# The first gate and value unit in two column halves, and the first weight clamp on GpSimd, in a chunked-scan and gated-MLP kernel

## The chip, the cores and the metric

The kernel runs on one core of a Trainium2 chip. A core has TensorE for matrix products (PE in the profile, its weight loads PEld), VectorE (DVE), ScalarE (ACT), GpSimd (POOL) and SyncE (SP), which here only issues DMAs. The metric is the device time of one execution in microseconds (us).

## What is computed

The reference is a decayed linear attention in chunks, followed by a gated MLP over its output. Cut to what matters:

```
cum = cumsum(log(clip(a)));  L = exp(cum_i - cum_j) * causal
y   = ((C B^T) * L) x  +  (C state) * exp(cum)          # within a chunk, and from the state carried in
state = exp(sum) * state + sum_j B_j x_j exp(cum_last - cum_j)
x   = y as [3072 tokens, 256]
out = (silu(x @ w_gate) * (x @ w_val)) @ w_out           # 256 -> 1536 -> 256
```

Batch 4, 8 heads, 768 positions, head size 32, state size 16; all data are float32.

## The kernel before

**Tiles and stages.** The 768 positions are cut into 6 blocks of 128 positions by 4 batches: 512 columns. A block's attention is done in pieces of Q=64 positions, so K=2 pieces in a block (the reference's chunk of 32 is not kept; the recurrence is the same). Its result y stands in four PSUM banks `y[2*q+g]`, where q is the piece and g the half of the 256 features, and is copied to SBUF as the MLP's moving operand: `xf` for block 0 (`x_whole`, line 510, four copies of 128x256), split into two parts for later blocks. The MLP works on 12 units f of 128 hidden features: `gate_val` (line 731) makes the bank `gv` of gate (m=0) and value (m=1) for a unit, `silu` and `product` combine them, `project` sums the output.

**Block 0** multiplies its first 9 units (WHOLE) in plain float32 with `w`, a rounded weight, instead of in three split products. A unit's weights come by DMA (`wg0r`, `wg1r`, ... 512 KB each) and go through six steps: `w_magnitude`, `w_sign`, `w_rest` on ScalarE; `w_range` (line 573, a clamp of 128x512), `w_shift` and `w_round` (lines 588 to 594) on VectorE. The unit can start when its `w_round` is done.

**Order of block 0.** Scan of the decays (`scan_spread`), scores S, `mix` (L times S, four instructions), `sums` (tile `st`, the new states, copied apart into T by ScalarE in `apart`), `values` (the part of y within a piece, in two groups g), `carried` (line 479, the part of y from the state, only for piece q=1), the four copies `xf`, and unit 0. `carried` needs the scan E and `weigh_c` (C times E, key `ce`). Between them TensorE runs `idle` products (tile `rest`, IDLE) so that it is not left without work.

**Block 1** is prepared meanwhile: its decays (`all`) are clamped by GpSimd in `clip_all`, written to DRAM by a DMA of ScalarE's queue (`write_all`, tile `clipped`) and read back, spread over partitions, as L and E by SP's queue (`load_aj`, `load_an`), along with `bc`, `xb` and the weights of units 7 to 11. VectorE scans L, weighs `xb` by it (`weigh_b`, key `bt`, one instruction for each batch) and TensorE then makes `st` and S of block 1.

**What sets the order.** The program is a list of steps (`add`), each with an engine and a cost, a rank, needs, and PSUM or SBUF slots that it takes. `Plan` simulates the engines with these costs and fixes each engine's instruction order once; at run time engines follow that order and wait on semaphores. `Ordered` holds each engine to program order. So a cost or rank that is changed for one step can move others. All recorded instructions carry line L199, a helper's; they are told apart by tiles.

Of the kernel before, what the change touches and what calls it, by code (L numbers as in the profile page):

```python
# [209 lines left out]
def scan_moe_kernel(ctx: ExitStack, tc, rows, decays, bc, xb, wgv, wo, cst, out):  # L210
# [635 lines left out]
    for n, ranks in enumerate(IDLE):  # L846
        for i, r in enumerate(ranks):
            need = [("idle", n, i - 1)] if i else [("idle", n - 1, len(IDLE[n - 1]) - 1)] if n else []
            if n:
                need = need + [(("S", 0, BATCH - 1), ("vals", 0), ("y", 0))[n - 1]]  # L850
            takes = [] if i or n else [("at", "rest")]
            c = T if n else P
            add("PE", 0.2133 * c / T, do(idle, n, i), r, need, takes=takes, uses=["rest"], gives=("idle", n, i), kind="r")


    for i in range(NW):
        r = due(0, i) - 1.0 if i < NF else due_sum(0, 2 * (i - NF)) - 1.0
# [4 lines left out]
        add([("Act", 0.57), ("DVE", 0.335)][: 1 + (i > 2)], None, do(w_rest, i), r - 4.5, [("mag", i), ("sign", i)], gives=("rest", i))
        add("Act", 0.57, do(w_sign, i), r - 5.4, [("mag", i)], gives=("sign", i))
        add("DVE", 0.6, do(w_shift, i), r - 4.2 if i else -1.05, [("range", i), ("sign", i)], gives=("shift", i))
        add("DVE", 0.6, do(w_round, i), r - 3.3 if i else -0.94, [("shift", i), ("rest", i), *([] if i else [("ce", 0)])], uses=[("raw", i)], gives=("round", i))
# [10 lines left out]
    add("Pool", 1.5, clip_all, 13.0, ["all", *(("bt", 0, b) for b in range(BATCH))], gives="clipped")  # L876
# [3 lines left out]
    for k in range(NB):  # L880
# [20 lines left out]
        if not k:  # L901
# [3 lines left out]
            for b in range(BATCH + 1):  # L905
                for i in range(2 if b < BATCH else 1):
# [7 lines left out]
                    need = [t, ("decays", 0), "dj"] + ([("scan0", b - last_one)] if i else []) + ([("M", 0, NP - 2)] if b == BATCH else [])  # L914
# [23 lines left out]
        for q in range(len(st)):  # L938
            add("Act", 0.5, do(apart, k, q), z + 4 + 0.5 * q, [("st", k, BATCH - 1), ("T", k)], uses=[st[q]], gives=("ap", k, q))
# [101 lines left out]
    for k in range(NB):  # L1041
        xs = [(t, k, i) for t in ("xh", "xl") for i in range(2 * K)]
        for f in range(NF):
# [10 lines left out]
            for m in range(2 if k < PAIR else 0):  # L1054
# [29 lines left out]
IDLE = [-9.0] * 22, [-1.45] * 4, [-1.35] * 2, [1000.0] * 3  # L1084
# [66 lines left out]
```

## Time and profile before

| | |
|---|---|
| three runs | 344.06, 345.26, 345.27 us; median 345.26 |
| profiled execution | 343.62 us, of which the span of instructions 341.9 us |
| PE busy | 337.3 us, 99% of the span |
| PEld, DVE, ACT, POOL busy | 260.7, 256.8, 173.4, 4.1 us |
| granted TensorE clock | 1.00 in every slice |
| bytes moved | 28.29 MB, mean 83 GB/s |

A busy share is an average over the kernel: TensorE is busy nearly all the time from 5.8 us on, VectorE without gaps worth the name only up to some 60 us, and the DMA engines mostly up to 39 us. The change lies in the first 20 us. So the timelines of the single engines in that stretch, and in block 1's preparation that follows it, are what is to be read, with the end of one instruction held against the start of the one that needs it.

### The profile page before, as it was taken

What the parts mean: (1) busy time and instruction counts of PE and PEld (TensorE: products, weight loads), DVE (VectorE), ACT (ScalarE), POOL (GpSimd) and SP (SyncE); (2) the same over time, 40 slices, a digit from 0 to 9 for tenths busy, and PEclk for the clock granted to TensorE, in tenths of its full rate; (3) what the DMA queues carried; (4) which work ended last, traced back from release to release, by engine and by line L of the source; (5) the groups of instructions that cost most, each with busy time, mean ns of one, the idle gap of its engine ahead of it and who ended that gap; (6) DMA issues with size and microseconds to landing.
All of it is one profiled execution on the core that took longest, in us unless ns stands there. A gap on an engine that the chain in (4) does not pass through costs nothing.

```text
span 341.9 us, 7521 instructions
## 1 busy us (share of the span) xinstructions
PE 337.3 (99%) x3165; PEld 260.7 (76%) x3165; DVE 256.8 (75%) x473; ACT 173.4 (51%) x315; POOL 4.1 (1%) x11
## 2 busy tenths in 40 slices
PE   8999999999999999999999999999999999999996
PEld 7544457888777888877788778877788888888895
DVE  6999999979697586553599943595869999856540
ACT  3696897372684552421344432323656556444542
POOL 1300000000000000000000000000000000000000
PEclk9999999999999999999999999999999999999999
DMA  7789535950000931000380107500010000000101
GB/s 257 259 263 334 176 120 173 220 172 1 0 2 15 254 108 62 0 2 2 124 191 0 63 2 206 105 2 2 3 63 0 0 3 0 0 0 2 51 11 63
DMA packets 10602, 28.29 MB, mean 83 GB/s; under 512 B 1096, under 2 KB 2120, under 8 KB 10568
## 3 DMA queue, kind: packets, MB, share of 16 engines
q1 hardware_dynamic: 10152, 27.57, 27.3%
q8 instruction: 25, 0.41, 0.5%
q10 hardware_dynamic: 416, 0.23, 0.2%
q14 instruction: 9, 0.07, 0.1%
HBM read 24.46 MB, written 3.35 MB: 81 GB/s over the span
## 4 chain that ended last, share of the span: by engine, by line
PE 89%; DMA 5%; ACT 4%; SPq 0%; issue 0%; ACTq 0%
PE gv L199 34%; PE po L199 30%; PE py L199 7%; PE y L199 5%; PE px L199 5%; DMA wg9r<-in_wgv 4%; PE pr L199 2%; PE pz L199 2%; PE S L199 2%; DMA bc<-in_bc 1%; PE st L199 1%; PE rest L199 1%; ACT sg L199 1%; ACT Cz L199 0%; ACT wg9r L199 0%; ACT wg2r L199 0%
## 5 line engine op out<-in xcount | busy, mean ns | idle before, releaser
L199 ACT CAST hh<-sg 128x512 fp32r<-128x512 f32 x70 | 43.4, 621 | 51.2 <-PE po L199 29.0
L199 DVE TENSOR_TENSOR hl<-sg,hh 128x512 fp32r<-128x512 f32 x72 | 49.3, 689 | 25.8 <-ACT hh L199 25.5
L199 ACT ACTIVATE sg<-gv 128x512 f32<-128x512 f32 x48 | 28.5, 595 | 50.6 <-PE gv L199 50.4
L199 DVE TENSOR_TENSOR sg<-gv,sg 128x512 f32<-128x512 f32 x48 | 32.8, 686 | 27.1 <-PE gv L199 27.0
L199 DVE TENSOR_TENSOR_SCAN L<-L,dj 128x520 f32<-128x520 f32 x20 | 23.9, 1227 | 0.0
L199 DVE TENSOR_TENSOR L<-S,L 128x512 f32<-128x512 f32 x24 | 15.0, 683 | 0.4 <-PE S L199 0.4
L199 PE MATMUL py<-xht,ws 128*128 128x512 f32 x48 | 14.8, 389 | 0.0
L199 ACT COPY ob<-po 128x512 f32<-128x512 f32 (+1 forms) x12 | 6.6, 551 | 13.1 <-PE po L199 12.5
L199 ACT ACTIVATE sg<-px 128x512 f32<-128x512 f32 x12 | 7.2, 598 | 10.9 <-PE px L199 10.9
L199 ACT ACTIVATE Cz<-bc,cs 128x512 f32<-128x512 f32 x12 | 8.0, 714 | 8.5 <-DMA bc<-in_bc 8.5
L199 DVE TENSOR_TENSOR mix<-mix 128x128 f32<-128x128 f32 (+1 forms) x36 | 11.9, 330 | 0.2
L199 DVE TENSOR_TENSOR ps<-py,ps 128x512 f32<-128x512 f32 x12 | 8.2, 686 | 4.8 <-PE py L199 4.8
L199 PEld LDWEIGHTS y<-L,xb 64*32 64x32 f32 x768 | 7.3, 105 | 5.0 <-issue 2.8
L199 PE MATMUL y<-L,xb 64*32 64x64 f32 x768 | 10.9, 222 | 0.0
L199 PEld LDWEIGHTS py<-xht,ws 128*128 128x128 f32 x48 | 9.0, 188 | 1.9
L199 PE MATMUL po<-hh,wo0h 128*128 128x512 f32 (+1 forms) x26 | 10.3, 394 | 0.0
L199 PE MATMUL po<-hh,wo2h 128*128 128x512 f32 (+1 forms) x26 | 9.9, 382 | 0.0
L199 PE MATMUL po<-hh,wo3h 128*128 128x512 f32 (+1 forms) x26 | 9.9, 381 | 0.0
L199 PE MATMUL y<-bc,T 32*64 32x64 f32 x352 | 9.9, 228 | 0.0
L199 PE MATMUL po<-hh,wo5h 128*128 128x512 f32 (+1 forms) x26 | 9.8, 378 | 0.0
L199 PE MATMUL po<-hh,wo4h 128*128 128x512 f32 (+1 forms) x26 | 9.8, 378 | 0.0
L199 PE MATMUL po<-hl,wo0h 128*128 128x512 f32 (+1 forms) x26 | 9.7, 375 | 0.0
(485 smaller groups left out, 875.0 us busy)
## 6 DMA issues: line engine op xcount, KB each, us to landing
L<-clipped SPq DMA_DIRECT2D x10, 520.0 KB, 9.7
xb<-in_xb SPq DMA_DIRECT2D x6, 768.0 KB, 5.1
bc<-in_bc SPq DMA_DIRECT2D x6, 512.0 KB, 9.2
out<-ob SPq DMA_DIRECT2D x11, 256.0 KB, 2.1
E<-clipped SPq DMA_DIRECT2D x5, 260.0 KB
wg0r<-in_wgv SPq DMA_DIRECT2D x1, 512.0 KB, 7.4
wg1r<-in_wgv SPq DMA_DIRECT2D x1, 512.0 KB
wg2r<-in_wgv SPq DMA_DIRECT2D x1, 512.0 KB, 4.2
```

The source lines that it names most:

```text
L199: ins = getattr(self.engine, name)(*a, **k)
```

## The change

Unit 0 of block 0 is multiplied by `gate_val_part` in four parts (gate or value, m, by column half q) with 256 columns each. A part of half q needs only the two copies of `xf` of that piece. The first part comes before `carried`, which now needs the first part to be issued, and the other three after it. `carried` no longer holds the banks of piece 0 (`y[:2]`). The second copy of piece 0 goes from ScalarE to VectorE. The clamp of `wg0` goes to GpSimd, ahead of `clip_all` there, which now needs it. E's scan and `weigh_c` come after `w_round` of unit 0 instead of before. Of the idle products there is one fewer before `sums` and one fewer between the two `values`, and the last three stand between the second `values` and unit 0's first part, no longer behind `carried`; costs and ranks of several steps are changed with it.

```diff
     def w_range(i):
         wf = part[i]["w"].bitcast(F32)
-        ve.tensor_scalar(wf, wf, *F32_RANGE, ALU.max, ALU.min)
+        (ve if i else ge).tensor_scalar(wf, wf, *F32_RANGE, ALU.max, ALU.min)
...
+    def gate_val_part(m, q):
+        if not q:
+            hid.setdefault((0, 0), {})["gv"[m]] = ps_mm.tile([P, T], F32, tag="mm", name=f"gv0_0_{m}")
+        t = hid[0, 0]["gv"[m]].rearrange("p (b i) -> p b i", b=BATCH)[:, :, piece(q)]
+        w = part[0]["w"].bitcast(F32).rearrange("p (a b c) -> p a b c", b=2, c=P)
+        for kc in range(2):
+            te.matmul(t, w[:, m, kc], x_part(whole[0], 2 * q + kc), start=not kc, stop=kc == 1, skip_group_check=True)
...
-        add("DVE", 0.335, do(w_range, i), r - 4.5 if i else -1.05, [("mag", i)] + ([("round", 0), *([("round", 1)] if i == 2 else [])] if i > 1 else []), gives=("range", i))
+        add(*(("DVE", 0.335) if i else ("Pool", 0.45)), do(w_range, i), r - 4.5 if i else -1.3, [("mag", i)] + ([("ce", 0)] if i == 1 else []) + ([("round", 0), *([("round", 1)] if i == 2 else [])] if i > 1 else []), gives=("range", i))
...
-    add("Pool", 1.5, clip_all, 13.0, ["all", *(("bt", 0, b) for b in range(BATCH))], gives="clipped")
+    add("Pool", 1.5, clip_all, 13.0, ["all", ("range", 0), *(("bt", 0, b) for b in range(BATCH))], gives="clipped")
...
-                    need = [t, ("decays", 0), "dj"] + ([("scan0", b - last_one)] if i else []) + ([("M", 0, NP - 2)] if b == BATCH else [])
+                    need = [t, ("decays", 0), "dj"] + ([("scan0", b - last_one)] if i else []) + ([("round", 0)] if b == BATCH else [])
...
-            add("PE", 0.135, do(carried, 0, b), -1, [("vals", 0), ("vals", 1), ("ce", 0), *steps], uses=uses, gives=("y", 0) if b == BATCH - 1 else ("y", 0, b), kind="f")
+            add("PE", 0.15, do(carried, 0, b), due(0, 0) + 0.05, [("gvp", 0), ("vals", 0), ("vals", 1), ("ce", 0), *steps], uses=[u for u in uses if u not in y[:2]], gives=("y", 0) if b == BATCH - 1 else ("y", 0, b), kind="f")
...
-                add([("Act", 0.62), ("DVE", 0.34)][i // 2 :][:1], None, do(x_whole, i), -0.9 + i / 10, [*(done if i > 1 else [("vals", 1)]), "xf"], uses=[y[i]], gives=("xf", i))
+                add([("Act", 0.62), ("DVE", 0.34)][min(i, 1) :][:1], None, do(x_whole, i), -1.0925 if i == 1 else -0.9 + i / 10, [*(done if i > 1 else [("vals", 1)]), "xf"], uses=[y[i]], gives=("xf", i))
...
+            for m, q in ((m, q) for q in range(K) for m in range(2 if not k and not f else 0)):
+                need = [("round", 0), ("xf", 2 * q), ("xf", 2 * q + 1), *([("gvp", m)] if q else []), ("idle", len(IDLE) - 1, len(IDLE[-1]) - 1)]
+                add("PE", 0.87, do(gate_val_part, m, q), r + q * 0.2 + m * 0.1, need + ([("y", 0)] if m and not q else []), takes=[] if q else [("mm", gv[m])], uses=[gv[m], "xf"] + ([("hh", "x")] if q else []), gives=gv[m] if q else ("gvp", m), kind="r")
...
-IDLE = [-9.0] * 22, [-1.45] * 4, [-1.35] * 2, [1000.0] * 3
+IDLE = [-9.0] * 22, [-1.45] * 3, [-1.35], [-1.3] * 3
```

On TensorE around unit 0, where `y_1_...<-bc` is `carried` and `gv_0_0`, `gv_0_1` are gate and value of unit 0, before:

```order
L199 MATMUL y_1_261<-bc_96,T_105 64x64
L199 MATMUL y_1_304<-bc_96,T_105 64x64
...
L199 LDWEIGHTS const-bfloat16-1.0
L199 MATMUL rest<-dn,const-bfloat16-1.0 128x512
...
L199 MATMUL gv_0_0_377<-xf,wg0w 128x512 x2
L199 MATMUL gv_0_1_392<-xf,wg0w 128x512 x2
L199 MATMUL gv_1_0_410<-xf,wg1w 128x512 x2
```

and now:

```order
L199 LDWEIGHTS const-bfloat16-1.0
L199 MATMUL rest<-dn,const-bfloat16-1.0 128x512
...
L199 MATMUL gv_0_0_344<-xf,wg0w 128x4x64 x2
L199 MATMUL y_1_259<-bc_96,T_105 64x64
L199 MATMUL y_1_301<-bc_96,T_105 64x64
...
L199 MATMUL gv_0_1_374<-xf,wg0w 128x4x64 x2
L199 MATMUL gv_0_0_344<-xf,wg0w 128x4x64 x2
L199 MATMUL gv_0_1_374<-xf,wg0w 128x4x64 x2
L199 MATMUL gv_1_0_403<-xf,wg1w 128x512 x2
```

The 16 products of `carried` moved from before the three idle products to behind the first half of the gate.

On VectorE from the end of `mix` to the rounding of unit 1 (`ISA` on a weight is `w_round`, the `SCALAR_TENSOR_TENSOR` on it `w_shift`, `bc_96<-bc_96,E_95` is `weigh_c`), before is - and now is +:

```order
-L199 SCALAR_TENSOR_TENSOR E_95<-a_0_202,dn 128x260
-L199 TENSOR_SCALAR wg0w<-wg0w 128x512
-L199 TENSOR_TENSOR bc_96<-bc_96,E_95 128x4x64
 L199 SCALAR_TENSOR_TENSOR wg0w<-wg0w,wg0r 128x512
 L199 ISA wg0w<-wg0r,wg0w 128x1024
...
+L199 COPY xf<-y_0_300 128x4x64
+L199 SCALAR_TENSOR_TENSOR E_95<-a_0_202,dn 128x260
+L199 TENSOR_TENSOR bc_96<-bc_96,E_95 128x4x64
```

E's scan and `weigh_c` went behind unit 0's rounding and a copy of `xf`, and the clamp of `wg0` is gone from this engine; the clamp of unit 1, the two other copies, `w_shift`, one cast and `w_round` of unit 1 follow in that order.

On SP, where L, E, `bc`, `xb` of block 1 are asked for, before is - and now is +:

```order
-L199 DMA L_367<-clipped 64x4x520 x2
-L199 DMA bc_389<-in_bc 128x1024
-L199 DMA xb_397<-in_xb 128x1536
+L199 DMA L_378<-clipped 64x4x520 x2
+L199 DMA E_379<-clipped 128x1x520
+L199 DMA bc_407<-in_bc 128x1024
+L199 DMA xb_412<-in_xb 128x1536
 L199 DMA wg7r<-in_wgv 128x1024
 L199 DMA wg8r<-in_wgv 128x1024
-L199 DMA E_368<-clipped 128x1x520
 L199 DMA wg9r<-in_wgv 128x1024
```

E of block 1 moved ahead of `bc`, `xb` and the weights of units 7 and 8.

## Rows read from the trace of the kernel before

**Rows 1.** The page, busy time, share of the span and instructions of each engine.

```profile
PE 337.3 (99%) x3165; PEld 260.7 (76%) x3165; DVE 256.8 (75%) x473; ACT 173.4 (51%) x315; POOL 4.1 (1%) x11
```

**Rows 2.** The timeline of PE around unit 0: start us, length us, engine, line, operation, tiles, shapes, count.

```profile
9.88 1.04 PE L199 MATMUL rest<-dn,const-bfloat16-1.0 128*128 128x512 bf16 x4
...
12.80 0.86 PE L199 MATMUL y<-L,xb 64*32 64x64 f32 x64
13.59 0.69 PE L199 MATMUL y<-bc,T 32*64 32x64 f32 x32
14.22 0.82 PE L199 MATMUL rest<-dn,const-bfloat16-1.0 128*128 128x512 bf16 x3
15.10 3.67 PE L199 MATMUL gv<-xf,wg0w 128*128 128x512 f32 x8
18.84 3.67 PE L199 MATMUL gv<-xf,wg1w 128*128 128x512 f32 x8
22.35 3.60 PE L199 MATMUL gv<-xf,wg2w 128*128 128x512 f32 x8
25.78 3.60 PE L199 MATMUL gv<-xf,wg3w 128*128 128x512 f32 x8
```

**Rows 3.** The timeline of DVE from `mix` to the rounding of unit 1 (the custom instruction is `w_round`), same columns; a length holds the drain, so that instructions overlap in the record.

```profile
9.45 2.46 DVE L199 TENSOR_TENSOR L<-S,L 128x512 f32<-128x512 f32 x4
11.83 0.69 DVE L199 TENSOR_TENSOR_SCAN E<-a,dn 128x260 f32<-128x260 f32 x1
12.43 0.41 DVE L199 TENSOR_SCALAR wg0w<-wg0w 128x512 f32<-128x512 f32 x1
12.74 0.42 DVE L199 TENSOR_TENSOR bc<-bc,E 128x256 f32<-128x256 f32 x1
13.08 0.70 DVE L199 SCALAR_TENSOR_TENSOR wg0w<-wg0w,wg0r 128x512 int32<-128x512 int32 x1
13.93 0.69 DVE L199 CUSTOM_DVE_ANT_0 wg0w<-wg0r,wg0w 128x1024 uint16<-128x1024 uint16 x1
14.54 0.75 DVE L199 COPY xf<-y 128x256 f32<-128x256 f32 x2
...
18.01 0.69 DVE L199 CUSTOM_DVE_ANT_0 wg1w<-wg1r,wg1w 128x1024 uint16<-128x1024 uint16 x1
```

**Rows 4.** The timeline of ACT in the same stretch, and the DMA of its queue (ACTq).

```profile
10.07 0.68 ACT L199 ACTIVATE wg0w<-wg0r 128x512 f32<-128x512 f32 x1 [2.02 <-DMA wg0r<-in_wgv]
10.78 0.70 ACT L199 ACTIVATE wg0r<-wg0r 128x512 int32<-128x512 int32 x1
11.72 0.62 ACT L199 ACTIVATE T<-st,cs 128x128 f32<-128x128 f32 x2 [0.24 <-PE st L199]
12.19 0.41 ACTq L199 DMA_DIRECT2D clipped<-all  x1
...
13.31 0.74 ACT L199 COPY xf<-y 128x256 f32<-128x256 f32 x2
```

**Rows 5.** The timeline of POOL, its work of more than 0.34 us.

```profile
0.88 0.66 POOL L199 TENSOR_SCALAR_AFFINE_SELECT rows<-const-float32-1.0 128x512 f32<-128x512 f32 x1 [0.39 <-POOLq L1140]
...
8.95 1.52 POOL L199 TENSOR_TENSOR xb<-xb,L 128x128 f32<-128x128 f32 x4 [7.13 <-DVE L L199]
10.66 1.49 POOL L199 TENSOR_SCALAR all<-all 128x384 f32<-128x384 f32 x1 [0.19 <-DMA all<-in_decays]
```

**Rows 6.** The timeline of SP's queue: when it asked for L of block 1 (two DMAs) and for the weights of unit 11, which the program lets go when L's second half has landed.

```profile
19.76 1.34 SPq L199 DMA_DIRECT2D L<-clipped  x2
...
28.65 0.33 SPq L199 DMA_DIRECT2D wg11r<-in_wgv  x1
```

**Rows 7.** Who SP's queue waited for: us in total, times, longest us.

```profile
SPq L199 <- DMA clipped<-all: 5.8, 1, 5.8
```

**Rows 8.** The timeline of DVE in block 1's preparation: the first scan of L, the first and the last `weigh_b`; in brackets the idle time before an instruction and who ended it.

```profile
28.90 1.24 DVE L199 TENSOR_TENSOR_SCAN L<-L,dj 128x520 f32<-128x520 f32 x1
...
31.60 0.29 DVE L199 TENSOR_TENSOR xb<-xb,L 128x128 f32<-128x128 f32 x1 [0.29 <-DMA xb<-in_xb]
...
38.35 0.29 DVE L199 TENSOR_TENSOR xb<-xb,L 128x128 f32<-128x128 f32 x1
```

**Rows 9.** The timeline of ACT there: the magnitudes of units 8 and 9, and block 1's states copied apart.

```profile
35.55 0.70 ACT L199 ACTIVATE wg8w<-wg8r 128x512 f32<-128x512 f32 x1 [0.69 <-DMA wg8r<-in_wgv]
...
38.21 0.68 ACT L199 ACTIVATE wg9w<-wg9r 128x512 f32<-128x512 f32 x1 [0.36 <-DMA wg9r<-in_wgv]
...
41.84 1.11 ACT L199 ACTIVATE T<-st,cs 128x128 f32<-128x128 f32 x4
```

**Rows 10.** The timeline of PE there: block 1's `st` and S.

```profile
39.61 0.86 PE L199 MATMUL st<-xb 64*32 64x64 f32 x64
...
42.31 1.85 PE L199 MATMUL S<-Cz,bc 32*64 32x128 f32 x64
```

**Rows 11.** The chain that ended last, one piece of it: start us, us, what.

```profile
43.01 1.16 PE S L199 x57
```

**Rows 12.** Busy time in a stretch: us from and to, its length, then PE, PEld, DVE, ACT, POOL busy us (instructions), granted PE clock, DMA share, GB/s.

```profile
13.60:17.00 3.40, 3.34 (x45) 1.73 (x41) 3.25 (x9) 2.28 (x5) 0.00 (x0) 1.00 0.98 354
```

**Rows 13.** The timeline near the kernel's end, two products of `project` with 256 columns in a row.

```profile
325.44 0.28 PE L199 MATMUL po<-hl,wo1h 128*128 128x256 f32 x1
...
325.55 0.28 PE L199 MATMUL po<-hh,wo1l 128*128 128x256 f32 x1
```

More of the change, by code (lines that the diff above doesn't have):

```diff
@@ L849, in scan_moe_kernel @@
             if n:
-                need = need + [(("S", 0, BATCH - 1), ("vals", 0), ("y", 0))[n - 1]]
+                need = need + [(("S", 0, BATCH - 1), ("vals", 0), ("vals", 1))[n - 1]]
             takes = [] if i or n else [("at", "rest")]
@@ L859, in scan_moe_kernel @@
         plan.marked[plan.ops[-1]] = ("sent", i)
-        add("Act", 0.565, do(w_magnitude, i), r - 5.5, [("raw", i)] + ([("xf", 2 * K - 1)] if i else []) + ([("rest", 1)] if i in (2, 3) else []), takes=[("sg" if i < NF else "w", ("w", i))], gives=("mag", i))
-        add("DVE", 0.335, do(w_range, i), r - 4.5 if i else -1.05, [("mag", i)] + ([("round", 0), *([("round", 1)] if i == 2 else [])] if i > 1 else []), gives=("range", i))
[L862 to L865, printed above, removed]
+        add("Act", 0.565, do(w_magnitude, i), r - 5.5, [("raw", i)] + ([("xf", 1 if i < 2 else 2 * K - 1)] if i else []) + ([("rest", 1)] if i in (2, 3) else []), takes=[("sg" if i < NF else "w", ("w", i))], gives=("mag", i))
+        add(*(("DVE", 0.335) if i else ("Pool", 0.45)), do(w_range, i), r - 4.5 if i else -1.3, [("mag", i)] + ([("ce", 0)] if i == 1 else []) + ([("round", 0), *([("round", 1)] if i == 2 else [])] if i > 1 else []), gives=("range", i))
+        add([("Act", 0.57), ("DVE", 0.335)][: 1 + (i > 2)], None, do(w_rest, i), r - 4.5 if i else -1.3, [("mag", i), ("sign", i)], gives=("rest", i))
+        add("Act", 0.57, do(w_sign, i), r - 5.4 if i else -1.2, [("mag", i)], gives=("sign", i))
+        add("DVE", 0.6, do(w_shift, i), r - 4.2 if i else -1.095, [("range", i), ("sign", i), *([("xf", 2 * K - 1)] if i == 1 else [])], gives=("shift", i))
+        add("DVE", 0.6, do(w_round, i), r - 3.3 if i else -1.094, [("shift", i), ("rest", i)], uses=[("raw", i)], gives=("round", i))
         early = WHOLE <= i < NF
@@ L933, in scan_moe_kernel @@
             n = len(bs)
-            add("PE", 0.11 if n == 1 else 0.787, do(sums, k, bs), -1.5 if not k else z + 3, [*(("bt", k, i) for i in bs), *([("st", k, more - 1)] if more else [] if k else [("spread", BATCH - 1, 1)])], takes=[] if more else [("at", i) for i in st], uses=st, gives=("st", k, b), kind="f", slack=SLACK, rows=1.0)
+            add("PE", 0.155 if n == 1 else 0.787, do(sums, k, bs), -1.5 if not k else z + 3, [*(("bt", k, i) for i in bs), *([("st", k, more - 1)] if more else [] if k else [("spread", BATCH - 1, 1)])], takes=[] if more else [("at", i) for i in st], uses=st, gives=("st", k, b), kind="f", slack=SLACK, rows=1.0)
             add("PE", 0.214 if n == 1 else 1.14, do(scores, k, bs), z + 3.5 if k else -1.9 + 0.1 * b, ([("Cz", k), ("st", k, BATCH - 1)] if k else apart_done) + ([("S", k, more - 1)] if more else []), takes=[] if more else [("at" if k else "mm", i) for i in S], uses=[*S, CZ], gives=("S", k, b), kind="f", slack=SLACK, rows=1.0)
@@ L938, in scan_moe_kernel @@
         for q in range(len(st)):
-            add("Act", 0.5, do(apart, k, q), z + 4 + 0.5 * q, [("st", k, BATCH - 1), ("T", k)], uses=[st[q]], gives=("ap", k, q))
+            add("Act", 0.5, do(apart, k, q), z + 4 + 0.5 * q, [("st", k, BATCH - 1), ("T", k), *([] if k else [("xf", 0) if q else ("rest", 0)])], uses=[st[q]], gives=("ap", k, q))
         for p in range(NP):
@@ L952, in scan_moe_kernel @@
             need = [("M", 0, p) for p in (2 * g, 2 * g + 1)]
-            add("PE", 0.45, do(values, 0, range(BATCH), (g,)), -1.4 + 0.1 * g, need, takes=[("mm", y[2 * q + g]) for q in range(K)], uses=[L, XB, *y], gives=("vals", g), kind="f")
+            add("PE", 0.62, do(values, 0, range(BATCH), (g,)), -1.4 + 0.1 * g, need, takes=[("mm", y[2 * q + g]) for q in range(K)], uses=[L, XB, *y], gives=("vals", g), kind="f")
         if k:
@@ L1053, in scan_moe_kernel @@
             gv = [("gv", k, f, m) for m in range(2)]
-            for m in range(2 if k < PAIR else 0):
+            for m, q in ((m, q) for q in range(K) for m in range(2 if not k and not f else 0)):
+                need = [("round", 0), ("xf", 2 * q), ("xf", 2 * q + 1), *([("gvp", m)] if q else []), ("idle", len(IDLE) - 1, len(IDLE[-1]) - 1)]
+                add("PE", 0.87, do(gate_val_part, m, q), r + q * 0.2 + m * 0.1, need + ([("y", 0)] if m and not q else []), takes=[] if q else [("mm", gv[m])], uses=[gv[m], "xf"] + ([("hh", "x")] if q else []), gives=gv[m] if q else ("gvp", m), kind="r")
+            for m in range(2 if k < PAIR and (k or f) else 0):
                 add("PE", c, do(gate_val, k, f, m), r + m * 0.1, need, takes=[("mm", gv[m])], uses=[gv[m], *([("x", k)] if k else ["xf", ("hh", "x")])], gives=gv[m], kind="r")
```

## The prediction

> **What bounds the kernel now.** The page first: TensorE is busy 99% of the span [rows 1], so the kernel is a queue of TensorE work, and a change in the first 20 us can only move the time by (a) when unit 0 starts, (b) gaps later in that queue. Second, TensorE's timeline around unit 0 [rows 2]: unit 0 starts at 15.10 and unit 1 at 18.84, a distance of 3.74, where units 2 and 3 lie 25.78 - 22.35 = 3.43 apart. So unit 1 came 0.31 late, and VectorE's timeline tells why: `w_round` of unit 1 runs from 18.01 to 18.70 [rows 3]. Unit 0 waits for the end of VectorE's list (clamp, `weigh_c`, shift, round, copies of `xf` to 15.29) [rows 3]. Third, where the queue stalls next: block 1's preparation. S of block 1 takes 1.85 us [rows 10], and the chain that ended last enters it only at 43.01 [rows 11], when ACT's copies of T (41.84 to 42.95) [rows 9] have freed the banks that `st` held. So some 43.01 - 42.31 = 0.7 us after S began, TensorE was still waiting for it. Whatever unit 0 gains must still be there at 43.01.
>
> **The head, part by part.** The changed order is laid on these durations; a hop between engines is taken as 0.1 us.
>
> GpSimd: the clamp of `wg0` can start when the magnitude ends, 10.07 + 0.68 = 10.75 [rows 4], so at 10.85. No row has a clamp of 128x512 on GpSimd. The bounds: not under 0.41, which is VectorE's own time for it [rows 3]; not over 1.49 x 512/384 = 1.99, which is `clip_all`, the same operation, by the element [rows 5]. I take 0.66, the pass over an unbroken 128x512 on the same engine [rows 5], because `clip_all` goes over 6 short rows and the clamp of `wg0` over one long one. Then the clamp ends at 11.51, before VectorE has done `mix` (11.83, where the next instruction starts [rows 3]): on this side it costs nothing. What it costs stands behind it in GpSimd's queue: `clip_all` starts at 11.5 instead of 10.66 and ends at 13.0 instead of 12.15, 0.85 later.
>
> One sentence from the notes for the near bound: the Trainium skill, GPSIMD Engine Reference, section 4.1 Engine selection, says that one-input work on GpSimd goes at about line rate; for 512 elements at its 1.2 GHz that would be an estimate of 0.43 us, and the sum below would be 0.2 us lower; no run here shows it.
>
> VectorE: shift at 11.83, round at 12.43, free at 13.03 (slots of 0.6, as 12.43 - 11.83 [rows 3]). The copy of `xf` needs the second `values`, which began at 12.80 and ended at 13.66 [rows 2]. Two idle products fewer stand ahead of it, 0.22 each (four fill 9.88 to 10.92 with their tail [rows 2]): it ends at 13.2. Copies to 13.65 (0.37 each [rows 4]). TensorE's three idle products (0.66) end at 13.9. So the first part starts at 13.9 instead of 15.10.
>
> TensorE from there: four parts of 3.43 / 4 = 0.86, and `carried`, 14.22 - 13.59 = 0.63 [rows 2], inside the unit: 13.9 to 14.75, `carried` to 15.4 (E's scan and `weigh_c` take 0.6 + 0.34 [rows 3] after 13.65 and are done at 14.6), second part to 16.25; the copies of piece 1 fall under it (15.5 to 16.2); end 17.95. Halves cost nothing extra by the row of `project`: two products with 256 columns start 0.11 apart [rows 13], though there in another number format; 0.02 us more on each of the 16 passes, which I take as the far bound, would be 0.3. Unit 1: VectorE is free at 16.2, then shift 0.6, cast 0.34, round 0.7 to 17.85. Unit 1 starts at 17.95 instead of 18.84: **0.9 us gained**, if nothing later waits.
>
> **What is late next.** `clip_all` feeds the DMA of `clipped`, which ACT's queue issued at 12.19, just after `clip_all` [rows 4, 5]; SP's queue waited 5.8 us for it before it could ask for L at 19.76 [rows 6, 7]. The DMA of `clipped` ran amid the fetches of the weights; I take it to land as much later as it is issued. So L is asked for at 20.6 instead of 19.76. L's second half landed at about 28.6 (unit 11's fetch is let go at 28.65 [rows 6]) and its scan started at 28.90, so it had no slack [rows 8]. Next, E stands ahead of `bc` and `xb` now. `xb` was waited for already: 0.29 us of idle time until 31.60 [rows 8]. E's 260 KB against L's 1040 KB in the 5 us or so before L's landing makes 1.2 us. So `xb` lands at 31.6 + 0.85 + 1.2 = 33.6. From the first to the end of the last `weigh_b` the new order has two scans (1.15 each), two products, shift and round (0.6 each), a clamp (0.33) and the four `weigh_b` (0.2 each), 5.8 us; before, the last began 38.35 - 31.60 = 6.75 after the first, with one scan more between [rows 8]. The last `weigh_b` is done at 39.4 and `st` starts at 39.5: about where it was before, 39.61 [rows 10]. TensorE, 0.9 early, waits 0.8 for it.
>
> Then S. ACT waited for the weights of units 8 and 9 (0.69 us until 35.55, 0.36 until 38.21 [rows 9]), and its chain to T begins with the latter: now 39.05 (E is ahead of them in both orders), while unit 8's, at 35.55 + 0.85 + 1.2 = 37.6, are done with by then. Five instructions of 0.5 to 0.6 follow (one fewer than before stands ahead of T) and T's 1.1: 39.05 + 2.8 + 1.1 = 42.95. T ended at 42.95 before [rows 9]. **Sum: the 0.9 us of the head is given back at `st`, and S goes on at 43.0 as before: 0.0 us**, within the errors of the hops. In the profiled execution that is 343.6 us (span 341.9); the median of the runs is 345.26, 1.64 above it, and I keep that distance: 345.2 us. Behind S both orders run TensorE without waits; VectorE's list to unit 9's low weights has lost a clamp, a cast and a shift (0.33 + 0.33 + 0.6), more than `st` and `mix` can be late, so nothing there should stall.
>
> **Rivals.**
>
> *The gain is kept.* The DMA of `clipped` may land at the same time as before, if what it waits for is the fetches ahead in the DMA engines and not its own issue. For: it took 19.76 - 12.19 = 7.6 us for 195 KB. Against: it is on another queue than the fetches. Then L is on time and only E delays `xb` (32.8): `st` 38.75, T done at 42.1, S goes on 0.9 earlier: 344.3 us.
>
> *Slower, by a slow clamp.* If GpSimd goes by the element as in `clip_all`, the clamp takes 1.99, ends at 12.85 and `clip_all` at 14.35. Shift and round slip by 1.1, and ACT's queue stands still at the issue of `clipped`, ahead of its copy of `xf`, until 14.4, so unit 0 starts at 15.2. L is asked for 2.2 later, T ends 1.3 later: 346.5 us. It decides from a clamp of about 0.7 us on: from there each 0.1 us of it costs 0.1.
>
> *GpSimd and VectorE block each other.* `clip_all` now runs beside `w_shift` and `w_round`, which read two tensors from SBUF. Before, it ran beside `mix`, which reads one from PSUM [rows 3, 5], and `weigh_b` kept its 0.4 there too: these rows don't show a conflict and can't rule one out. If VectorE's shift has to wait for the whole of `clip_all`, it starts at 13.0, unit 0 at 14.8 and unit 1 at 18.9: no gain in the head, and `st` and S where the late L puts them anyway, so 345.3 us; the end is the forecast's, by another way. This is a rule of the Trainium skill, SBUF — State Buffer, section Who interferes with whom: a VectorE instruction with two SBUF inputs contends with a GpSimd instruction that reads SBUF, and the one that comes second is blocked whole. By that rule the head gains nothing.
>
> *The clock.* TensorE was granted 1.00 through the stretch, with PE 3.34 of 3.40 us busy [rows 12]. The new order leaves no long gap there; if the grant fell to 1.2 GHz for one unit, 3.43 us more. Little speaks for it.
>
> **How the numbers follow.** Forecast (given back, 345.2, by itself 344.7 to 345.8) 0.48; kept, 344.3, 0.20; slow clamp, 346.5, 0.17; blocking, 345.3, 0.10; clock and what I have not seen 0.05, mostly slower. 0.5%, some 1.7 us, is about what a measurement of this kernel can tell from no change, and three runs of one kernel already lie 1.2 us apart. Below 343.5 lies only a kept gain with a median that fell low: 0.06. Above 347.0 lie the last case and the tail of the slow clamp: 0.09. The range takes in both bounds of the clamp and the kept gain, with half the spread of the runs at each side: 343.7 to 347.0.
>
> **What would show it.** Right: first part of unit 0 near 13.9 and unit 1 near 18.0; GpSimd's clamp near 0.7 us; `clipped` issued near 13.0 and L asked for near 20.6; a wait of TensorE of 0.5 to 1 us ahead of `st` for `weigh_b`; S going on near 43.0. Wrong: L asked for at 19.8 (gain kept), a clamp over 1 us (slow clamp), a shift that starts when `clip_all` ends (blocking), or a wait of TensorE between 44 and 62, where VectorE's list moved too and I rely on its slack.

## The result

| | before | changed |
|---|---|---|
| median of 14 runs each | 344.91 us (343.22 to 347.28) | 346.78 us (345.83 to 348.19) |
| ratio | 1 | 1.0062, 95% interval [1.0041, 1.0083] |
| profiled execution, its span | 343.62, 341.9 us | 346.5, 344.8 us |

The change made the kernel slower by 0.62%, with an interval of 1.4 to 2.9 us; the medians lie 1.87 us apart. The forecast was no change (345.2). The time lies inside the range, close to that of the rival "slower, by a slow clamp" (346.5).

**One correction first.** The spans differ by 2.9 us, but 0.76 of that lies ahead of anything that was changed: `mix` begins at 10.21 instead of 9.45 [rows 3]. That start varies from profile to profile with the same code (9.50 to 10.28 in the others of this study). So what follows is told from the start of `mix` on; 2.9 - 0.76 = 2.14 us is left, about what the timed runs show.

GpSimd of the changed kernel, the timeline (rows 5 answer to it; columns as there):

```profile
10.87 1.92 POOL L199 TENSOR_SCALAR wg0w<-wg0w 128x512 f32<-128x512 f32 x1
12.86 2.00 POOL L199 TENSOR_SCALAR all<-all 128x384 f32<-128x384 f32 x1
```

The clamp takes 1.92 us, not 0.66, and `clip_all` behind it 2.00 instead of 1.49 [rows 5]. Together GpSimd is done at 14.86.

ACT, the timeline (rows 4, and at the end rows 9):

```profile
12.28 0.62 ACT L199 ACTIVATE T<-st,cs 128x128 f32<-128x128 f32 x2 [0.20 <-PE st L199]
14.89 0.39 ACTq L199 DMA_DIRECT2D clipped<-all  x1
15.32 0.37 ACT L199 COPY xf<-y 128x256 f32<-128x256 f32 x1 [2.42 <-POOL all L199]
...
44.30 1.10 ACT L199 ACTIVATE T<-st,cs 128x128 f32<-128x128 f32 x4
```

ACT has to issue the DMA of `clipped` between its copies, so its whole queue stands for 2.42 us until `clip_all` is done, and the copy of `xf` with it.

VectorE, the timeline (rows 3):

```profile
10.21 2.46 DVE L199 TENSOR_TENSOR L<-S,L 128x512 f32<-128x512 f32 x4
12.82 0.69 DVE L199 SCALAR_TENSOR_TENSOR wg0w<-wg0w,wg0r 128x512 int32<-128x512 int32 x1
13.66 0.76 DVE L199 CUSTOM_DVE_ANT_0 wg0w<-wg0r,wg0w 128x1024 uint16<-128x1024 uint16 x1
14.34 0.41 DVE L199 COPY xf<-y 128x256 f32<-128x256 f32 x1
```

VectorE itself loses little here: the shift begins 0.03 after the clamp's end (12.79), and `mix` fills the time up to about 12.6. That is luck of this profile, in which the clamp starts early, 0.66 after `mix` began. In E late of experiment 6, with the same order around it, the clamp starts 1.22 after `mix` began (11.16 - 9.94), VectorE stands 0.68 for it, and unit 1 is 1.09 later than before instead of 0.52. In the changed kernel's profile VectorE's copy of `xf` is done at 14.75; ACT's begins only at 15.32.

TensorE around unit 0, the timeline (rows 2), and from `st` of block 1 on (rows 10):

```profile
15.75 1.13 PE L199 MATMUL gv<-xf,wg0w 128*128 128x256 f32 x4 [0.75 <-ACT xf L199]
16.81 0.69 PE L199 MATMUL y<-bc,T 32*64 32x64 f32 x32
17.43 2.86 PE L199 MATMUL gv<-xf,wg0w 128*128 128x256 f32 x12
20.12 3.60 PE L199 MATMUL gv<-xf,wg1w 128*128 128x512 f32 x8
...
40.82 0.72 PE L199 MATMUL st<-xb 64*32 64x64 f32 x48
42.83 0.35 PE L199 MATMUL st<-xb 64*32 64x64 f32 x16 [1.28 <-DVE xb L199]
43.10 1.99 PE L199 MATMUL gv<-xf,wg7w 128*128 128x512 f32 x4
45.02 1.59 PE L199 MATMUL S<-Cz,bc 32*64 32x128 f32 x64
46.53 1.98 PE L199 MATMUL gv<-xf,wg7w 128*128 128x512 f32 x4
...
53.52 0.73 PE L199 MATMUL gv<-xh,wg9h 128*128 128x512 f32 x2
54.34 0.73 PE L199 MATMUL gv<-xh,wg9l 128*128 128x512 f32 x2
...
63.96 0.62 PE L199 MATMUL gv<-xh,wg0h 128*128 128x512 f32 x2
```

SP's queue, the timeline (rows 6), and VectorE's first scan of L, first and last `weigh_b` (rows 8):

```profile
23.05 1.35 SPq L199 DMA_DIRECT2D L<-clipped  x2
24.50 0.68 SPq L199 DMA_DIRECT2D E<-clipped  x1
25.29 0.35 SPq L199 DMA_DIRECT2D bc<-in_bc  x1
25.68 0.42 SPq L199 DMA_DIRECT2D xb<-in_xb  x1
...
30.94 0.33 SPq L199 DMA_DIRECT2D wg11r<-in_wgv  x1
```

```profile
30.96 1.24 DVE L199 TENSOR_TENSOR_SCAN L<-L,dj 128x520 f32<-128x520 f32 x1 [0.51 <-DMA L<-clipped]
...
36.87 0.29 DVE L199 TENSOR_TENSOR xb<-xb,L 128x128 f32<-128x128 f32 x1 [2.33 <-DMA xb<-in_xb]
...
42.48 0.28 DVE L199 TENSOR_TENSOR xb<-xb,L 128x128 f32<-128x128 f32 x1
```

Two points of before that the rows ahead don't hold, TensorE's value half of unit 7 and the first unit of block 1, from the timeline of PE of the kernel before:

```profile
44.09 1.98 PE L199 MATMUL gv<-xf,wg7w 128*128 128x512 f32 x4
...
61.06 0.62 PE L199 MATMUL gv<-xh,wg0h 128*128 128x512 f32 x2
```

Laid from the start of `mix` (9.45 before, 10.21 changed), in us:

| point | before | changed | later by |
|---|---|---|---|
| `clipped` issued | 2.74 | 4.68 | 1.94 |
| unit 0 begins | 5.65 | 5.54 | -0.11 |
| unit 1 begins | 9.39 | 9.91 | 0.52 |
| L asked for | 10.31 | 12.84 | 2.53 |
| L landed (fetch of unit 11) | 19.20 | 20.73 | 1.53 |
| first `weigh_b` | 22.15 | 26.66 | 4.51 |
| `st` begins | 30.16 | 30.61 | 0.45 |
| S begins | 32.86 | 34.81 | 1.95 |
| value half of unit 7 | 34.64 | 36.32 | 1.68 |
| block 1's unit 0 | 51.61 | 53.75 | 2.14 |

Read down TensorE's points: half a microsecond is lost by unit 1 (instead of 0.9 gained); `st` then waits 1.28 us for the last `weigh_b`, whose `xb` landed late (it was asked for 3.14 us later than before, behind L and E). The start of the waiting products costs some 0.2 more. S gives 0.27 back (its 0.27 us of waiting before, 44.09 - 42.31 = 1.78 against 46.53 - 45.02 = 1.51, is gone). The low weights of unit 9 take 0.25 (54.34 - 53.52 = 0.82, against 51.56 - 50.99 = 0.57 in the timeline of before): VectorE's list now makes the low part of `xf` (`hlx`, at 52.99) directly ahead of them, which it did at 17.41 before. The rest is in small pieces. From there to the end nothing changes: 2.14 at block 1, 2.14 at the span's end.

### The profile page after: what moved, and what is told of

Its sections match the earlier page's. It is cut to its first block, busy times and chain, and to the rows that moved or that the text cites. A ratio compares the mean times of both kernels' runs of the same rounds, so it can differ in the third digit from the quotient of the medians.

```text
span 344.8 us, 7527 instructions
## 1 busy us (share of the span) xinstructions
PE 338.1 (98%) x3168; PEld 262.9 (76%) x3171; DVE 258.0 (75%) x474; ACT 171.6 (50%) x313; POOL 6.7 (2%) x12
## 3 DMA queue, kind: packets, MB, share of 16 engines
HBM read 24.46 MB, written 3.35 MB: 81 GB/s over the span
## 4 chain that ended last, share of the span: by engine, by line
PE 83%; DVE 3%; issue 1%; ACT 0%; ACTq 0%
PE gv L199 31%; PE po L199 29%; PE py L199 7%; PE px L199 5%; PE y L199 4%; PE pr L199 2%; PE pz L199 2%; PE S L199 1%; PE st L199 1%; DVE L L199 1%; DVE wg8w L199 0%; DVE T L199 0%; DVE wg9w L199 0%; DVE wg9l L199 0%; DVE sg L199 0%
```

## Experiments

**The theory** (A in the expectations): the clamp on GpSimd is the cause; 1.92 us ahead of `clip_all` puts `clipped`, L, `bc` and `xb` of block 1 too late. **The rivals**, which the expectations word and price run by run: the column halves or the new order on VectorE cost the time themselves; E's new place does; or the clamp harms in another way than by making `clip_all` late (a late weight of unit 0, a conflict of the engines).

Every ratio is against the kernel before on the same chip, with its 95% interval, from five rounds unless said.

**1. The clamp alone** (before, with the clamp of `wg0` on GpSimd; nothing in halves). The cut leaves out the line of `add` that gives the clamp its engine, cost and rank. E is asked for behind `xb` but ahead of the weights of units 7 and 8, so its place is not quite that of before.

```diff
-        ve.tensor_scalar(wf, wf, *F32_RANGE, ALU.max, ALU.min)
+        (ve if i else ge).tensor_scalar(wf, wf, *F32_RANGE, ALU.max, ALU.min)
...
-    add("Pool", 1.5, clip_all, 13.0, ["all", *(("bt", 0, b) for b in range(BATCH))], gives="clipped")
+    add("Pool", 1.5, clip_all, 13.0, ["all", ("range", 0), *(("bt", 0, b) for b in range(BATCH))], gives="clipped")
```

> The kernel before with the clamp of wg0 on GpSimd ahead of clip_all, and nothing else of the change (unit 0 whole, carried ahead of it; in SP's queue E comes to stand between xb and the weights of unit 7). Theory A: the clamp takes 1.9 us, L is asked for 2 to 2.5 us later, TensorE waits ahead of or in st, and the time is 1.3 to 2.5 us above the kernel before. Theory B: within 0.5 us of the kernel before.

Measured: 347.30 us, **1.0071 [1.0051, 1.0091]**. The timelines of POOL and of PE in this run:

```profile
10.78 1.92 POOL L199 TENSOR_SCALAR wg0w<-wg0w 128x512 f32<-128x512 f32 x1 [0.36 <-ACT wg0w L199]
12.78 2.00 POOL L199 TENSOR_SCALAR all<-all 128x384 f32<-128x384 f32 x1
```

```profile
40.37 0.72 PE L199 MATMUL st<-xb 64*32 64x64 f32 x48
42.76 0.35 PE L199 MATMUL st<-xb 64*32 64x64 f32 x16 [1.67 <-DVE xb L199]
...
46.01 1.66 PE L199 MATMUL S<-Cz,bc 32*64 32x128 f32 x60 [0.62 <-ACT T L199]
```

As theory A expected: the same 1.92 and 2.00, a wait of 1.67 ahead of `st`, and as great a loss within the noise, without any column halves. So the halves aren't needed for the loss.

**2. All but the clamp** (the changed kernel with the clamp on VectorE, behind `mix`):

```diff
-        (ve if i else ge).tensor_scalar(wf, wf, *F32_RANGE, ALU.max, ALU.min)
+        ve.tensor_scalar(wf, wf, *F32_RANGE, ALU.max, ALU.min)
...
-        add(*(("DVE", 0.335) if i else ("Pool", 0.45)), do(w_range, i), r - 4.5 if i else -1.3,
+        add("DVE", 0.335, do(w_range, i), r - 4.5 if i else -1.096,
...
-    add("Pool", 1.5, clip_all, 13.0, ["all", ("range", 0), *(("bt", 0, b)
+    add("Pool", 1.5, clip_all, 13.0, ["all", *(("bt", 0, b)
```

> The changed kernel with the clamp of wg0 on VectorE again, behind mix; the column halves and the rest stay, and TensorE's order is the changed one. Theory A (the clamp takes 1.9 us on GpSimd, so clip_all, the DMA of clipped, L and xb of block 1 come late, and TensorE waits for weigh_b in st): clip_all is back at about 1.5 us and starts some 0.5 us after weigh_b, SP's queue asks for L about 2.5 us earlier than in the changed kernel, no wait of over 0.5 us in st, and the time is 1.5 to 2.7 us below the changed kernel, so 0.3 to 0.8 us below the kernel before or level with it. Theory B (the column halves and the moved scan of E cost the time in the head): the time stays within 0.7 us of the changed kernel.

Measured: 345.15 us, 1.0023 [1.0000, 1.0047]. `clip_all` is back at 1.49 us and L is asked for at 19.88; the planner put E between `bc` and `xb`, and SP's queue stood 3.3 us behind `bc` until it could ask for E (see 6). Its profile holds an idle time of 1.58 us inside unit 0 that no other profile here has and that nothing in it explains, so the place of its 0.8 us is not read from this trace.

**3. The same with E behind the fetch of unit 8,** as before:

```diff
-            add("SP", 0.48, do(load_an, k), z - 9, ["written", ("decays", k), *late, *gate("an")], gives=("an", k), lag=1.3)
+            add("SP", 0.48, do(load_an, k), z - 9, ["written", ("decays", k), *late, *gate("an"), *([("sent", 8)] if k == 1 else [])], gives=("an", k), lag=1.3)
```

> As the run before, and E of block 1 is asked for behind the weights of unit 8 again, as in the kernel before (the order of VectorE in block 1's preparation moves with that). Theory A: xb lands 1.2 to 2 us earlier than with E ahead of it, so the gain of the head (0.5 to 0.9 us) is kept: 0.5 to 1.0 us below the kernel before. Theory B: within 0.7 us of the changed kernel.

Measured: 344.27 us, **0.9998 [0.9979, 1.0017]**. The halves, with the clamp on VectorE and E behind the fetch of unit 8, change nothing that can be measured: no loss, and no gain either; 0.5 to 1.0 us less than before had been expected. The planner moved other steps with them: on TensorE the gate half of unit 7 now stands ahead of `st` of block 1 and its value half ahead of S. So this is no run of the halves with all else as before. TensorE's timeline of this run (its `mix` began at 9.50):

```profile
12.96 0.86 PE L199 MATMUL y<-L,xb 64*32 64x64 f32 x64 [0.25 <-issue]
13.98 0.59 PE L199 MATMUL rest<-dn,const-bfloat16-1.0 128*128 128x512 bf16 x2 [0.16 <-issue]
14.41 1.03 PE L199 MATMUL gv<-xf,wg0w 128*128 128x256 f32 x4
15.45 0.69 PE L199 MATMUL y<-bc,T 32*64 32x64 f32 x32
16.08 2.86 PE L199 MATMUL gv<-xf,wg0w 128*128 128x256 f32 x12
18.77 3.60 PE L199 MATMUL gv<-xf,wg1w 128*128 128x512 f32 x8
```

Unit 0 starts 4.91 after `mix`, 0.74 earlier than before (5.65), but unit 1 at 9.27 is only 0.12 earlier than before (9.39): the unit with `carried` in it lasts 18.77 - 14.41 = 4.36. The price of the two one after the other was 3.43 + 0.63 = 4.06; the 3.74 between the units before held 0.31 in which unit 1 came late. So the halves do start TensorE earlier, carry `carried` inside instead of ahead, and take 0.30 more than the sum. The 0.12 is lost again where TensorE waits for unit 9's low weights (51.73 - 50.80 = 0.93, against 0.57 before): block 1's unit 0 begins 0.2 us later after `mix` than before.

**4. `clip_all` first, then the clamp** (the changed kernel, GpSimd's two passes exchanged): the decays of block 1 on time, unit 0's weight late. The planner also put E between `bc` and `xb`, as in experiment 2 and not as in the changed kernel.

```diff
-        add(*(("DVE", 0.335) if i else ("Pool", 0.45)), do(w_range, i), r - 4.5 if i else -1.3, [("mag", i)]
+        add(*(("DVE", 0.335) if i else ("Pool", 0.45)), do(w_range, i), r - 4.5 if i else -1.3, [("mag", i)] + ([] if i else ["clipped"])
...
-    add("Pool", 1.5, clip_all, 13.0, ["all", ("range", 0), *(("bt", 0, b)
+    add("Pool", 1.5, clip_all, 13.0, ["all", *(("bt", 0, b)
```

> The changed kernel with clip_all ahead of the clamp of wg0 in GpSimd's queue. Theory A: L is asked for about when the kernel before asks for it, but the clamp ends only near 14.2, so unit 0 starts near 15.9 and unit 1 near 20 (both from a head as in the kernel before): the wait in st falls under 0.5 us, and the time is 0.5 to 1.5 us above the kernel before, below the changed kernel. Theory B: within 0.7 us of the changed kernel. If clip_all takes 1.5 us here and 2.0 in the changed kernel, it is slowed there by what runs beside it (w_shift and w_round of unit 0), and if it takes 2.0 here too, it is not.

Measured: 345.34 us, 1.0021 [1.0003, 1.0040]. POOL and VectorE in its timelines:

```profile
10.56 1.49 POOL L199 TENSOR_SCALAR all<-all 128x384 f32<-128x384 f32 x1 [0.20 <-DMA all<-in_decays]
12.13 1.92 POOL L199 TENSOR_SCALAR wg0w<-wg0w 128x512 f32<-128x512 f32 x1
```

```profile
14.08 0.69 DVE L199 SCALAR_TENSOR_TENSOR wg0w<-wg0w,wg0r 128x512 int32<-128x512 int32 x1 [2.09 <-POOL wg0w L199]
```

The clamp takes 1.92 us again while VectorE stands idle for it, so its price is its own and no conflict. Unit 1 is 1.5 us late here (20.38 against a `mix` at 9.50), later than in the changed kernel, and yet the time is better (1.0021 against 1.0062, the intervals just miss each other): a late unit 0 is largely made up before `st`, which waits for nothing in this run; a late `clip_all` is not. E's other place may have a part in that. With the same place of E and `clip_all` on time, experiment 2 measured 1.0023.

**5. `clip_all` twice** (before, the same clamp of the decays done a second time, which changes no value; every order is that of before):

```diff
-        clip(bl[0]["all"].rearrange("p i a t -> p (i a) t")[:, :, 1:], ge)
+        for _ in range(2):
+            clip(bl[0]["all"].rearrange("p i a t -> p (i a) t")[:, :, 1:], ge)
```

> The kernel before with clip_all done twice in a row on GpSimd (the second pass changes no value); every other instruction and its order are those of the kernel before. It makes the decays of block 1 late by one pass, 1.5 us, and leaves the head alone. If lateness of L and xb is what costs (theory A), SP's queue asks for L 1.5 us later, TensorE waits in st or in S, and the time is 0.7 to 1.6 us above the kernel before. If the clamp's cost lies in the head, in w_shift that waits for GpSimd (theory C), the time stays within 0.4 us of the kernel before.

Measured: 347.39 us, **1.0076 [1.0050, 1.0102]**, 2.6 us (1.7 to 3.5) for one pass more of 1.54 us, more than the 0.7 to 1.6 that were expected; part of it goes with a lower clock in four of its seven runs (see the clock below). Laid from `mix`, `clipped` was issued only 1.03 us later than before. ACT and PE in its timelines (`mix` began at 9.89):

```profile
13.66 0.42 ACTq L199 DMA_DIRECT2D clipped<-all  x1
...
44.56 1.12 ACT L199 ACTIVATE T<-st,cs 128x128 f32<-128x128 f32 x4
```

```profile
43.22 0.43 PE L199 MATMUL S<-Cz,bc 32*64 32x128 f32 x4
45.22 1.67 PE L199 MATMUL S<-Cz,bc 32*64 32x128 f32 x60 [1.56 <-ACT T L199]
```

Two costs add up: ACT's last step on `wg0` stands behind the issue of `clipped`, so VectorE's rounding waits 0.63 us and unit 1 is 0.5 late; and behind the late L, SP's queue asks late for the weights of units 7 to 9 (unit 9's 31.07 us after `mix` instead of 28.76). ACT waits for these and comes to T only at 44.56, so S waits 1.56 us for T. `xb` is late too (the first `weigh_b` waited 1.34), but `st` did not wait for it. Block 1's unit 0 begins 2.3 us later after `mix` than before. The two passes took 3.08 us in a row, 1.54 each, so it is not by following another GpSimd instruction that `clip_all` took 2.00. So no other harm of the clamp is needed: lateness of `clip_all` alone, with the clamp of `wg0` on VectorE, costs as much as the whole change, within the noise.

**6. E's place alone,** in two kernels. In the kernel before, E's DMA is put directly behind L's; in the changed kernel, directly behind the fetch of unit 8. Nothing else moves.

```diff
-        for op, e, t in self.order():
+        out = self.order()
+        at = {o[0].gives: i for i, o in enumerate(out)}
+        moved = out.pop(at["an", 1])
+        at = {o[0].gives: i for i, o in enumerate(out)}
+        out.insert(at["aj", 1] + 1, moved)    # changed kernel: at["raw", 8] + 1
+        for op, e, t in out:
```

> The kernel before with one DMA moved in SP's queue: E of block 1 is asked for right behind L, ahead of bc, xb and the weights of units 7 and 8, as in the changed kernel; all else in its order. If E's place costs by itself (theory A's second part), xb lands 1.2 to 2 us later, the last weigh_b ends 1 to 1.5 us later, st waits for it, and the time is 0.3 to 1.2 us above the kernel before. If it matters only when L is late as well, the time stays within 0.3 us.

> The changed kernel with one DMA moved in SP's queue: E of block 1 is asked for behind the weights of unit 8 as in the kernel before; all else in its order, the clamp on GpSimd among it. Theory A: xb lands 1.2 to 2 us earlier than in the changed kernel, the wait of 2.3 us ahead of the first weigh_b falls below 1 us, the one in st below 0.3 us, and the time is 0.5 to 1.5 us below the changed kernel, still above the kernel before, by the L that stays late. If E's place doesn't matter, it is that of the changed kernel within 0.4 us.

Measured: E first in the kernel before, 345.76 us, 1.0027 [1.0006, 1.0049]; E late in the changed kernel, 345.97 us, 1.0045 [1.0024, 1.0066] (the changed kernel itself 1.0062 [1.0041, 1.0083]: the intervals overlap). SP's queue in the first of the two:

```profile
20.61 1.35 SPq L204 DMA_DIRECT2D L<-clipped  x2
23.50 0.68 SPq L204 DMA_DIRECT2D E<-clipped  x1
...
24.69 0.42 SPq L204 DMA_DIRECT2D xb<-in_xb  x1
```

and VectorE's state steps of block 0 (the edit adds five lines, so that the helper's line is L204):

```profile
22.61 0.87 DVE L204 SCALAR_TENSOR_TENSOR T<-T,E 128x64 f32<-128x64 f32 x4
```

E's own DMA is one part; the other is that SP stands for 1.5 us (21.96 to 23.50) before it can issue it, and `bc` and `xb` behind it. E of block 1 goes into the buffer that E of block 0 holds, and VectorE reads that until 23.48 (22.61 + 0.87): SP asks for E 0.02 later. The first `weigh_b` comes 24.18 after `mix` (34.46 - 10.28), 2.0 later than before, and `st` waits 0.39. In the changed kernel SP has no such pause, since `clipped` is late anyway. With E moved back there the first `weigh_b` comes 24.38 after `mix` instead of 26.66, the wait ahead of `st` is gone, and S waits 0.48 for T instead. In time this run can't be told from the changed kernel. That what is left comes from the clamp fits the other runs; this run alone doesn't show it.

**7. The clamp between the second and third instruction of `mix`,** on VectorE, else as 3 (rank -1.12 instead of -1.096), an attempt at a better version:

```diff
-        add("DVE", 0.335, do(w_range, i), r - 4.5 if i else -1.096,
+        add("DVE", 0.335, do(w_range, i), r - 4.5 if i else -1.12,
```

> The column halves with the clamp on VectorE between the second and third mix instruction, and E of block 1 asked for late as in the kernel before: what should be left of the change without GpSimd. The clamp no longer stands between mix and w_shift, so unit 0 starts 0.2 to 0.4 us earlier than with the clamp behind mix, and unit 1 some 0.3 us earlier than in the kernel before. If that survives the preparation of block 1, the time is 0.2 to 0.6 us below the kernel before; if VectorE's list up to the low weights of unit 9 takes it back (TensorE waits there for wg9l, 0.5 us in the run with the clamp behind mix), it is the kernel before within 0.3 us.

Measured: 345.29 us, 1.0020 [1.0000, 1.0041]. Not better than 3, nor than before; 0.2 to 0.6 us less than before had been expected. S waits 0.60 us for T in its profile. No kernel of the study beat the kernel before.

**8. One operation instead of two** (as 4, but the clamp of `wg0` on GpSimd takes the lower bound alone; the upper one is left out):

```diff
-        (ve if i else ge).tensor_scalar(wf, wf, *F32_RANGE, ALU.max, ALU.min)
+        ve.tensor_scalar(wf, wf, *F32_RANGE, ALU.max, ALU.min) if i else ge.tensor_scalar(wf, wf, F32_RANGE[0], None, ALU.max)
```

> The changed kernel with GpSimd's clip_all ahead of the clamp of wg0 (as in clip_all_first), and the clamp of wg0 doing the lower bound alone (max; the min is left out, on this unit's weights only). Theory A: GpSimd's price is a pass over the elements, whatever the instruction does to each: 1.92 us again (1.8 to 2.0). Rival B: each of the two arithmetic operations has its own price, so that one of them takes 1.0 to 1.3 us. Time: by A as clip_all_first (345.3), by B 0.5 us less; one look can't tell these apart, the length of the instruction can.

A single run, 345.4 us beside 343.71. POOL's timeline:

```profile
10.96 1.50 POOL L199 TENSOR_SCALAR all<-all 128x384 f32<-128x384 f32 x1 [0.17 <-DMA all<-in_decays]
12.54 1.49 POOL L199 TENSOR_SCALAR wg0w<-wg0w 128x512 f32<-128x512 f32 x1
```

1.49 us: neither 1.92 nor 1.0 to 1.3. The second operation costs 0.43 of the 1.92; most of the price is the pass over the elements.

## Why the prediction missed

**The step that failed** is the price of the clamp: "I take 0.66, the pass over an unbroken 128x512 on the same engine". It measured 1.92, near the far bound of 1.99, which had been worked out by the element from `clip_all`. The nearest row by shape was an affine select; the nearest by operation was `clip_all`, two arithmetic operations on each element. By the element `clip_all` takes 1490 / 384 = 3.88 ns and the clamp 1920 / 512 = 3.75: the reason given against that row, six short rows against one long one, is worth next to nothing. The near bound, VectorE's 0.41, is further off. Beside it stood the Trainium skill, GPSIMD Engine Reference, section 4.1 Engine selection, with one-input work at about line rate, an estimate of 0.43 us. The trace does not agree with it, 1.92 us, or 1.49 with a single operation, and the measurement decides.

**What that did** is what the rival said, in its steps and nearly in its times. "ACT's queue stands still at the issue of `clipped`, ahead of its copy of `xf`, until 14.4": laid on before's start it stood until 14.89 - 0.76 = 14.13. "Unit 0 starts at 15.2": 14.99. "L is asked for 2.2 later": 2.53. "T ends 1.3 later": 44.30 + 1.10 - 0.76 = 44.64 against 42.95, 1.7. "346.5 us": 346.78; that is closer than it should be, since the rival added 1.24 us to a median of three runs, 345.26, and the change added 1.87 to one of 14, 344.91. Two of its parts were off. VectorE's shift slipped by 0.23, not 1.1, nearly all of that because the clamp could start as early as 0.66 after `mix` began in this profile, against 1.40 by the forecast (10.85 - 9.45), so the small loss in the head is luck (E late of experiment 6 shows the other case). And "each 0.1 us of it costs 0.1" is too mild where the delay goes through both queues: beyond 0.7 us the clamp took 1.22 more, and the change cost 1.87, the 0.5 of `clip_all` included.

**The gain of the head** would not have been 0.9 with a cheap clamp either. With the clamp on VectorE (experiment 3) unit 1 gains 0.12. Of the missing 0.78, 0.46 lies ahead of unit 0 (4.91 after `mix` began instead of 13.9 - 9.45 = 4.45), and the working is off in two places there. "Two idle products fewer stand ahead of it, 0.22 each": the second `values` was to come 0.44 earlier for that, and came 3.46 after the start of `mix`, against 12.80 - 9.45 = 3.35 before [rows 2]. TensorE's weight loads stand still inside the first `values` there. The timeline of PEld, of before and of experiment 3:

```profile
11.44 0.73 PEld L199 LDWEIGHTS y<-L,xb 64*32 64x32 f32 x63
```

```profile
12.37 0.18 PEld L199 LDWEIGHTS y<-L,xb 64*32 64x32 f32 x14 [0.43 <-issue]
12.64 0.10 PEld L199 LDWEIGHTS <-const-bfloat16-1.0 128*128 128x128 bf16 x1
```

Before, no pause of 0.1 us or more; in experiment 3 0.43 us, for which the profile names no cause. (The last line is the idle product between the two `values`; PE's timeline of the run lacks its record.) Over the runs with the changed order of TensorE's head the second `values` came 3.17 to 3.83 after `mix` began, with pauses of 0.16 to 0.71; over those with the order of before 3.35 to 3.74, with 0 to 0.33. So at a like pause it did come earlier with fewer idle products, and in experiment 3 the pause took that back. Why there is a pause stays open. VectorE would not have been ready sooner here either: its copy of `xf` runs from 13.91 to 14.33, behind a clamp that takes 0.58 us until the shift starts and a round that starts 0.84 after the shift, where the forecast took 0.60 from two instructions that don't need each other. The other 0.30 lies in the unit: 4.36 instead of 4.06. The far bound of 0.02 us for each half pass was "0.3", and the 12 passes in a row take 2.69 us, 0.224 each against 3.43 / 16 = 0.214; the first four, ahead of `carried`, 1.04 instead of 0.86.

**What comes late next** had the right places. A wait of TensorE ahead of `st` for `weigh_b` came, 1.28 us instead of 0.8, with an `xb` that was 4.5 later and not 2.05 (0.85 + 1.2): the clamp is part of it, and E's place is the other, taken as 1.2 and 2.0 in experiment 6, where SP's own pause counts in. A `clipped` that is issued 1.94 later was asked for as L 2.53 later: "as much later as it is issued" was the right side, and "the gain is kept" fell. ACT's chain to T did not begin with unit 9's weights, as the forecast had it, but with unit 7's, for which ACT waited 1.36 us until 38.08; from there it was busy up to T. And "nothing there should stall", of unit 9's low weights, was wrong by the 0.25 us above.

**S** was read too high. The chain of waits entered it 0.7 us after its start [rows 11], which was taken as 0.7 us of slack. The comparison with the changed kernel, where S runs through, shows 0.27.

**Blocking** didn't come as told: VectorE's shift didn't wait for `clip_all`. It was the other way round. `clip_all` begins 0.04 us after the shift in the changed kernel, in experiment 1 (12.78 against 12.73) and in E late of experiment 6 (13.15 against 13.11), and it takes 2.00 us in all three; where it doesn't start beside the shift it takes 1.49 to 1.54. The 0.5 us is about what is left of the shift then. That fits the rule of the Trainium skill, SBUF — State Buffer, section Who interferes with whom, by which the second of the two waits for the first. The rule's other half, that a VectorE instruction with two inputs that comes second is blocked until `clip_all` ends, does not show: `w_round` ran from 13.66 inside it, 0.76 instead of 0.69 us long, and in experiment 1 `weigh_c`, with two inputs, from 13.34 inside it, 0.73 instead of 0.42. No run took the shift away to settle it, so the cause of these 0.5 us is argued and not shown. They add to the clamp's delay.

**The clock** stayed at 1.00, 2.4 GHz, in the profiled execution, as forecast. Not so in all timed runs: the four longest of the 14 of the changed kernel (347.29 to 348.19 us) have a mean granted clock of 0.995. So have four of seven in experiment 5, three of eleven with E late in experiment 6 and one of six in experiment 1, all kernels with a late `clip_all`, and one of the 58 runs of the kernel before that were timed beside the experiments. No kept profile is of such a run, so where the clock fell is not known. It is a part of the loss that the forecast gave a small chance, but not most of it: the other ten runs of the changed kernel have a median of 346.58, still 1.67 above 344.91, and the other three of experiment 5 one of 346.47 beside 344.58.

## What to carry to other kernels

Price an operation on another engine by a row of the same operation, by the element, before a row of the same shape. Moving work to an idle engine is free only if what stands behind it in that engine's queue, and behind the DMA that waits for it in a third engine's queue, has slack: here an engine that is busy 2% of the span set the time, because the next block's loads hung on it. A unit that starts earlier is worth only what is still early at the next wait, so compare two traces from the last unchanged point, at one place after another along the bounding engine.

## What the runs showed of the hardware

- GpSimd's clamp of float32 with two operations: 1.92 us for 128x512, 1.49 for 128x384, 1.49 for 128x512 with one operation; VectorE takes 0.40 to 0.49 for 128x512 (0.63 once, inside `mix`, in experiment 7). From the three of GpSimd an estimate: 0.2 us for the instruction and 3.36 ns for each element of a partition, of which the second operation is 0.84.
- VectorE starts an instruction later when it needs the result of the one just before it: `w_round` 0.84 us after the start of `w_shift` (0.85 in [rows 3]), against 0.60 from the `w_shift` of unit 1 to the independent cast behind it (18.22 to 18.82 in the changed kernel); the shift 0.58 after the clamp's start in experiment 3, against 0.31 for `weigh_c` after the same clamp [rows 3].
- L was asked for 2.53 us later and landed 1.53 later. The hops of a chain through DMAs can't simply be added; that the later transfer met less traffic is likely, and was not tried.
- The sixteen 128x260 products at the kernel's start took 5.56 us in the changed kernel's profile and 4.24 in that of before, with the same code and a granted clock of 1.00 in both. No run was made to find out why.
